# Two-stage kernel (mLSTM cell, then hash routing): output gates as exp(-o) inside the divisor, and a prologue whose first gate rows move within SBUF

## The chip, the cores and the metric

The kernel runs on one core of a Trainium2 chip. The metric is the device time of one launch in microseconds (us); the kernel before takes 426.49 us (median of three runs, 426.43 to 426.7). Its profiled execution spans 423.8 us on the core.

Engine names in the profile: PE is TensorE (matmul), PEld its weight load, DVE is VectorE, ACT is ScalarE, POOL is GpSimd, SP is SyncE, which here only issues DMAs. A name with q (ACTq, SPq) is an engine's queue when it issues a DMA.

## The reference

Two blocks in a row. The first is an mLSTM cell over 4 batches, 8 heads, 768 time steps and head width 40; the second sends each of the 3072 rows to one of 8 experts (two matmuls with a ReLU between), chosen by a hash of the token's id.

```python
for t in range(S):
    m_new  = np.maximum(f_gate[:, :, t] + m, i_gate[:, :, t])
    f_stab = np.exp(f_gate[:, :, t] + m - m_new)
    i_stab = np.exp(i_gate[:, :, t] - m_new)
    m = m_new
    C = f_stab * C + i_stab * outer(v_t, k_t)        # per head, 40 x 40
    n = f_stab * n + i_stab * k_t
    h_tilde = C @ q_t
    denom = np.maximum(np.abs(n . q_t), 1.0)
    o = 1.0 / (1.0 + np.exp(-o_gate[:, :, t]))
    y[:, :, t] = o * h_tilde / denom
...
x = y.transpose(0, 2, 1, 3).reshape(B * S, H * D)    # 3072 x 320
out[rows of expert e] = np.maximum(x[rows] @ w1[e], 0) @ w2[e]
```

What matters here is the last line of the loop: the sigmoid of the output gate times the cell's output, divided by `denom`. Written out it is h_tilde / ((1 + exp(-o_gate)) * denom), one quotient.

## The kernel before

The time axis of the first block is cut into 24 steps `s` of 128 rows: 4 batches `b` with 6 chunks `c` each. In a step, TensorE turns k and q (transposes), computes the decay matrix from rows `R` and `L` of bf16 pieces (`decays`), the state (`state`), the scores q·k (`scores`) and the output (`attend`), and turns the output back (`back`); ScalarE takes the exp of the decays and copies PSUM to SBUF; VectorE weighs the scores; then `finish` divides and gates. The second block follows, TensorE's two large matmul loops (lines 836, 829 and 865 of the program). The program's order is each engine's order (`manual_schedule`).

The decay rows need the gates' running sums with full precision in bf16 operands, so each f32 row is split into three bf16 pieces. The pieces (`zA` for the decays A and exp(A), `zE` for the input side) are stored in DRAM and loaded back in the layout of `R` and `L`:

```python
def store_a(r, eng):   eng.dma_start(za_d[z_rows(r), :3, :], zA[r, :3, :])
def store_e(r, eng):   eng.dma_start(ze_d[z_rows(r)], zE[r])
def store_x(r, eng):   eng.dma_start(za_d[z_rows(r), 3:, :], zA[r, 3:, :])

def decays(s):
    ...
    for hf in range(2):
        ab = ps.tile([P, PR, P], F32, name="ab", tag="tr", bufs=4)
        for i in range(2):
            nc.tensor.matmul(ab[i * HB : (i + 1) * HB],
                lhsT=Ls[b % 2][:, c * P + i * HB : c * P + (i + 1) * HB],
                rhs=R[:, i, hf::2, :], start=True, stop=True)
        nc.scalar.activation(w[:, hf], ab[:], AF.Exp)

def sigmoid(s):
    o = og[s, "all"]                  # a group of 3 or 6 steps
    nc.scalar.activation(o, o, AF.Sigmoid)

def finish(s):
    d = st.pop(s)
    hs = d["xo"].rearrange("p f i (x d) -> p f (i x) d", d=DP)
    den = wk.tile([P, 2, PR, 1], F32, name="den")
    nc.vector.tensor_scalar(den[:], hs[:, :, :, D:D1], scalar1=-1.0, scalar2=1.0, op0=ALU.mult, op1=ALU.max)
    nc.vector.tensor_tensor(den[:], den[:], hs[:, :, :, D:D1], op=ALU.max)
    x = wk.tile([P, H, D], F32, name="x")
    xv = x.rearrange("p (j f) d -> p f j d", f=2)
    nc.vector.tensor_tensor(xv, hs[:, :, :, :D], og[s].rearrange("p (j f) d -> p f j d", f=2), op=ALU.mult)
    nc.vector.reciprocal(den[:], den[:])              # 128 x 8
    eng = nc.vector if s + 1 == NT else nc.gpsimd
    eng.tensor_tensor(xv, xv, den[:].to_broadcast([P, 2, PR, D]), op=ALU.mult)
    return lambda: nc.sync.dma_start(x_d[s * P : (s + 1) * P, :], x.rearrange("p h d -> p (h d)"))
```

The prologue (cut to its order): `g0` are 32 partitions with the first two chunks of all batches, `g1` 64 partitions with the other four.

```python
f_sb, i_sb <- gates (ACT queue);  k0, q0, k1, q1, v0, k2 (SP queue);  fP, iP (ACT queue)
tables()                                   # constant rows of R and L
scan of m, first 256 columns               # VectorE
turn_k(0); turn_q0(0)
load_q0(2), load_o(0), load_v(1), load_o(1), load_v(2), load_o(2)
scores(0)
gates(g0, ..., (G, G, G)); gates_e(g0, (A, A, A))     # pieces on GpSimd, ScalarE
store_a(g0, A); store_e(g0, A)
turn_k(1); turn_q0(1)
scan of m, the other 512 columns; m_sb -> mP by DMA
load_a(0, A); load_e(0, [0])               # R and L of step 0, from DRAM
gates_rest(g0, ...); store_x(g0, A)        # exp(A) and its pieces
...
gates_turn(g0); decays(0); entering(0); load_a(1, A); k_weights(0)
gates(g1, ...); weigh(0); ...; gates_e(g1, ...); store_a, store_e, gates_rest, store_x of g1
for s in range(NT): ...                    # the steps
```

Of the kernel before, what the change touches and what calls it, by code (L numbers as in the profile page):

```python
# [17 lines left out]
P = 128  # L18
# [4 lines left out]
def kernel(  # L23
# [93 lines left out]
    with tc.tile_pool(name="gates", bufs=1) as gp, \  # L117
# [48 lines left out]

        groups = [(0, 3)] + [(s, min(s + 6, NT)) for s in range(3, NT, 6)]
        og = {}

        def load_o(s):  # L170
            for s0, s1 in groups:
                if s == s0:
                    tile_o = ld.tile([P, 6, H, D], F32, name="og", bufs=2)
                    og[s, "all"] = tile_o[:, : s1 - s0]
                    for i in range(s0, s1):
                        og[i] = tile_o[:, i - s0]
            nc.sync.dma_start(og[s], rows_of(o_gate, s))

        def load_q(b, part):

            if part == 0:
                qb[b] = {"l": ld.tile([P, H, NB * D], F32, name="ql", bufs=2)}
            hs = slice(part * PR, (part + 1) * PR)
            nc.sync.dma_start(qb[b]["l"][:, hs], q[b, hs].rearrange("h (p r) d -> p h (r d)", r=NB))

# [19 lines left out]
        def pieces_of(z, i0, t, ra, rb, r, eng):  # L205
            for j, piece in enumerate((hi(t[r]), hi(ra[r]), rb[r])):
                if eng[j] is nc.scalar:
                    nc.scalar.copy(z[r, i0 + j, :], piece)
                else:
                    nc.gpsimd.tensor_copy(z[r, i0 + j, :], piece)  # L210

        def gates(rows, m0, m1, f, i, eng):

            r = rows
            first = r.start == 0
            nc.vector.tensor_add(aP[r], f, m0)
            nc.vector.tensor_sub(aP[r], aP[r], m1)
            if first:
                nc.vector.memset(aP[r, 0:1], 0.0)
            nc.gpsimd.tensor_tensor(iP[r], i, m1, op=ALU.subtract)  # L220
            nc.vector.tensor_tensor_scan(AP[r], keep[r], aP[r], 0.0, op0=ALU.mult, op1=ALU.add)
            nc.vector.tensor_tensor(r1[r], AP[r], hi(AP[r]), op=ALU.subtract)
            nc.vector.tensor_sub(iP[r], iP[r], AP[r])
            nc.vector.tensor_tensor(r2[r], r1[r], hi(r1[r]), op=ALU.subtract)
            pieces_of(zA, 0, AP, r1, r2, r, eng)
# [4 lines left out]
        def gates_e(rows, eng):  # L230
            r = rows
            nc.vector.tensor_tensor(r3[r], iP[r], hi(iP[r]), op=ALU.subtract)
            nc.vector.tensor_tensor(r4[r], r3[r], hi(r3[r]), op=ALU.subtract)
            pieces_of(zE, 0, iP, r3, r4, r, eng)

        def store_a(r, eng):
            eng.dma_start(za_d[z_rows(r), :3, :], zA[r, :3, :])
# [4 lines left out]
        def store_x(r, eng):  # L242
            eng.dma_start(za_d[z_rows(r), 3:, :], zA[r, 3:, :])

        def gates_rest(rows, eng):
            r = rows
            Ac = AP[r].rearrange("p (c t) -> p c t", t=P)
            n = r.stop - r.start
            nc.vector.tensor_tensor(
                aP[r].rearrange("p (c t) -> p c t", t=P), iP[r].rearrange("p (c t) -> p c t", t=P),  # L250
                Ac[:, :, P - 1 : P].to_broadcast([n, 2, P]), op=ALU.add,
            )
            nc.scalar.activation(fP[r], AP[r], AF.Exp)
            nc.scalar.activation(aP[r], aP[r], AF.Exp)
            nc.vector.tensor_tensor(r1[r], fP[r], hi(fP[r]), op=ALU.subtract)
            nc.vector.tensor_tensor(r2[r], r1[r], hi(r1[r]), op=ALU.subtract)
            pieces_of(zA, 3, fP, r1, r2, r, eng)
# [83 lines left out]
        def sigmoid(s):  # L341
            o = og[s, "all"]
            nc.scalar.activation(o, o, AF.Sigmoid)
# [81 lines left out]

        def finish(s):
            d = st.pop(s)
            hs = d["xo"].rearrange("p f i (x d) -> p f (i x) d", d=DP)
            den = wk.tile([P, 2, PR, 1], F32, name="den")
            nc.vector.tensor_scalar(  # L430
                den[:], hs[:, :, :, D:D1], scalar1=-1.0, scalar2=1.0, op0=ALU.mult, op1=ALU.max,
            )
            nc.vector.tensor_tensor(den[:], den[:], hs[:, :, :, D:D1], op=ALU.max)
            x = wk.tile([P, H, D], F32, name="x")
            xv = x.rearrange("p (j f) d -> p f j d", f=2)
            nc.vector.tensor_tensor(
                xv, hs[:, :, :, :D], og[s].rearrange("p (j f) d -> p f j d", f=2), op=ALU.mult,
            )
            nc.vector.reciprocal(den[:], den[:])  # L439
            eng = nc.vector if s + 1 == NT else nc.gpsimd  # L440
            eng.tensor_tensor(xv, xv, den[:].to_broadcast([P, 2, PR, D]), op=ALU.mult)  # L441
            return lambda: nc.sync.dma_start(x_d[s * P : (s + 1) * P, :], x.rearrange("p h d -> p (h d)"))
# [172 lines left out]
        first_turns = {1: (0,), 2: (1,), 3: (2,), 4: (3, 4), 5: (5,)}  # L615
# [26 lines left out]
        flat = {id(t): src.rearrange("b h s -> (b h) s") for t, src in ((f_sb, f_gate), (i_sb, i_gate), (fP, f_gate), (iP, i_gate))}  # L642
        nc.scalar.dma_start(f_sb[:], flat[id(f_sb)])
        nc.scalar.dma_start(i_sb[:], flat[id(i_sb)])
# [6 lines left out]
        load_q0(1)  # L651
        load_v(0)
        load_k(2)
        for i in (1, 2):
            for t in (fP, iP):
                nc.scalar.dma_start(t[at[i] : at[i] + BH, :], flat[id(t)][:, i * W2 : (i + 1) * W2])
        nc.vector.memset(m_sb[:, 0:1], 0.0)
        tables()
        for t in [ks[2], kws[0]]:
            nc.gpsimd.memset(t[:, :, D:], 0.0)  # L660
        nc.vector.memset(keep[:], 1.0)
        nc.vector.memset(keep.rearrange("p (c t) -> p c t", t=P)[:, :, 0:1], 0.0)
        g0, g1 = slice(0, BH), slice(2 * BH, 4 * BH)
        A, G = nc.scalar, nc.gpsimd
# [3 lines left out]
        turn_k(0)  # L668
        turn_q0(0)
        load_q0(2)  # L670
        load_o(0)
        load_v(1)
        load_o(1)
        load_v(2)
        load_o(2)
        scores(0)
        gates(g0, m_sb[:, :W2], m_sb[:, 1 : W2 + 1], f_sb[:, :W2], i_sb[:, :W2], (G, G, G))
        gates_e(g0, (A, A, A))
        store_a(g0, A)
        store_e(g0, A)  # L680
        turn_k(1)
        turn_q0(1)
        nc.vector.tensor_tensor_scan(
            m_sb[:, W2 + 1 :], f_sb[:, W2:], i_sb[:, W2:], m_sb[:, W2 : W2 + 1], op0=ALU.add, op1=ALU.max,
        )
        for i in (1, 2):
            nc.scalar.dma_start(mP[at[i] : at[i] + BH, :], m_sb[:, i * W2 : (i + 1) * W2 + 1])
        load_a(0, A)
        load_e(0, [0])
        gates_rest(g0, (G, G, G))  # L690
        store_x(g0, A)
        nc.gpsimd.memset(Rs[1][32:HB], 0.0)
        for r in (slice(0, 32), slice(HB, P)):
            nc.sync.dma_start(Rs[1][r], Rs[0][r])
        for t in vs:
            nc.gpsimd.memset(t[:, :, D1:], 0.0)
            nc.gpsimd.memset(t[:, :, D:D1], 1.0)
        load_q(1, 0)
        load_q(1, 1)
# [307 lines left out]
```

## Time and profile before

| | before |
|---|---|
| time, median of 3 | 426.49 us |
| span of the profiled execution | 423.8 us |
| first block (to the first matmul of line 924) | 165.1 us |
| scores (sp) of steps 0, 1, 2 start at | 9.60, 29.31, 38.05 us |
| a step of the first block after that | 5.0 to 6.9 us |
| ACT_TABLE_LOAD | 5 before Sigmoid, 5 before the next Exp, 1 at the start; 1.28 us each |
| DVE reciprocal, 128x8 | 24 of 0.193 us |
| POOL product x·den, 128x320 | 23 of 0.724 us |

In the profile's second part the span is cut into 40 slices of 10.6 us; each digit is an engine's busy share in tenths. In the table of stretches each engine has its busy time in us, with the number of its instructions in brackets, then come the granted clock of TensorE as a share of full speed, the mean busy share of the 16 DMA engines, and GB/s. In the timeline a row has start and duration in us, engine, line, operation, and in square brackets the idle time ahead of it with what ended that. In a list of groups a row has the line, engine, operation, tiles, shapes and count; then the busy time in us and the mean of one in ns; then idle time and what ended it.

### The profile page before, as it was taken

The page shows a single profiled execution, that of the slowest core. Times are in us where ns is not written, and L with a number is a line of the kernel's source. Part 1 is how long each engine was busy: PE and PEld are TensorE (multiplying, and loading weights), DVE is VectorE, ACT ScalarE, POOL GpSimd, SP SyncE. Part 2 cuts the span into 40 slices and gives each one's busy share as a digit, 9 for nine tenths or more (in the row PEclk, how much of TensorE's full clock was granted, in tenths as well). Part 3 has the DMA queues.
Part 4 walks back from the last instruction along what each step waited for, and adds up shares of the span by engine and source line. Part 5 has one row for each costly group of instructions (what it writes and reads, how often), then busy time and mean ns, then how long its engine had stood idle before and what let it go on. Part 6 is the DMA issues. An engine that isn't in the chain of part 4 may idle for free.

```text
span 423.8 us, 7461 instructions
## 1 busy us (share of the span) xinstructions
PE 392.1 (93%) x2892; PEld 262.1 (62%) x2892; DVE 136.2 (32%) x373; ACT 134.3 (32%) x238; POOL 117.7 (28%) x202
## 2 busy tenths in 40 slices
PE   2369999999999997999999999999999999999992
PEld 2247877877887874556657556556556566575551
DVE  7364748776675762220120110210110201201100
ACT  5158786696495471010111111110111101111010
POOL 6364313313433421711402401311302212020021
PEclk9988999999999999999999999999999999999998
DMA  9829998899675630548508217144126100000000
GB/s 173 212 61 177 205 206 188 191 207 223 153 163 126 162 95 33 151 147 254 168 26 263 87 62 224 63 125 160 60 96 185 62 17 29 0 17 30 0 18 30
DMA packets 111784, 51.37 MB, mean 121 GB/s; under 512 B 86624, under 2 KB 105892, under 8 KB 111748
## 3 DMA queue, kind: packets, MB, share of 16 engines
q1 hardware_dynamic: 105898, 39.31, 38.2%
q0 software_dynamic: 2496, 8.20, 6.0%
q10 hardware_dynamic: 3354, 3.37, 2.4%
q8 instruction: 23, 0.38, 0.4%
q14 instruction: 13, 0.11, 0.1%
HBM read 42.00 MB, written 8.63 MB: 119 GB/s over the span
## 4 chain that ended last, share of the span: by engine, by line
PE 84%; ACT 5%; issue 5%; POOL 2%; DVE 1%; ACTq 1%; DMA 1%; POOLq 0%; DVEq 0%
PE mh L836 22%; PE zp L865 21%; PE sp L351 7%; PE ht L409 6%; PE mh L829 6%; PE ht L402 3%; PE mh L924 3%; PE ab L311 2%; PE tr L275 2%; PE xo L424 2%; PE ht L382 2%; PE tr L288 2%; PE tk L589 2%; PE tp L811 1%; PE xb L323 1%
## 5 line engine op out<-in xcount | busy, mean ns | idle before, releaser
L865 PE MATMUL zp<-w2t,h 128*128 128x320 f32 x384 | 105.2, 433 | 0.0
L836 PE MATMUL mh<-xT,w1t 128*128 128x416 f32 x256 | 96.2, 519 | 0.5 <-issue 0.5
L865 PEld LDWEIGHTS zp<-w2t,h 128*128 128x128 f32 x384 | 72.7, 190 | 32.1 <-issue 3.3
L836 PEld LDWEIGHTS mh<-xT,w1t 128*128 128x128 f32 x256 | 46.7, 190 | 42.7 <-issue 41.6
L817 DVE COPY xT<-tp 128x384 f32<-128x384 f32 x16 | 8.9, 558 | 141.4 <-PE tp L813 98.1
L798 POOL DMA_INDIRECT out_dram<-zo,s_idx x26 | 25.7, 988 | 92.5 <-ACT zo L797 92.5
L845 ACT ACTIVATE h<-mh 128x416 f32<-128x416 f32 x32 | 16.6, 517 | 107.4 <-PE mh L829 54.7
L797 ACT COPY zo<-zp 128x320 f32<-128x320 f32 x26 | 11.1, 426 | 101.1 <-PE zp L865 92.9
L843 DVE TENSOR_SCALAR h<-mh 128x416 f32<-128x416 f32 x32 | 18.9, 592 | 52.1 <-PE mh L829 26.3
L359 DVE TENSOR_TENSOR w<-sp,w 128x512 f32<-128x512 f32 x48 | 30.9, 686 | 13.7 <-PE sp L351 10.3
L441 POOL TENSOR_TENSOR x<-x,den 128x320 f32<-128x320 f32 x23 | 16.6, 724 | 61.6 <-DVE den L439 29.6
L351 PE MATMUL sp<-qT,kT 64*128 64x128 f32 x384 | 29.7, 297 | 4.1 <-ACT qT L289 4.1
L351 PEld LDWEIGHTS sp<-qT,kT 64*128 64x128 f32 x384 | 24.9, 199 | 10.7 <-ACT qT L289 5.9
L315 ACT ACTIVATE w<-ab 128x512 f32<-128x512 f32 x48 | 26.8, 614 | 4.6 <-PE ab L311 4.6
L409 PE MATMUL ht<-w,v 128*64 128x128 f32 x384 | 27.1, 285 | 0.0
L791 POOL DMA_INDIRECT xg<-x_rows,g_idx x24 | 23.4, 974 | 12.6 <-issue 12.6
L829 PE MATMUL mh<-xT,w1c 64*128 64x416 f32 x128 | 26.7, 535 | 0.0
L952 POOL COPY hrem<-h 128x256 f32<-128x256 f32 x8 | 3.2, 400 | 81.9 <-ACT h L845 81.9
L417 ACT COPY hT<-ht 128x512 f32<-128x512 f32 x24 | 14.1, 587 | 31.2 <-PE ht L409 31.2
L409 PEld LDWEIGHTS ht<-w,v 128*64 128x64 f32 x384 | 21.2, 140 | 4.0 <-issue 3.1
L289 ACT COPY qT<-tr 128x512 f32<-128x512 f32 x24 | 22.9, 977 | 0.6 <-PE tr L288 0.3
L275 PE MATMUL tr<-ident,k 128*128 128x128 f32 x96 | 17.4, 309 | 4.1 <-POOL R L638 4.1
(181 smaller groups left out, 421.3 us busy)
## 6 DMA issues: line engine op xcount, KB each, us to landing
w2t<-in_moe_w_dram SPq DMA_DIRECT2D x28, 320.0 KB
w1t<-in_moe_w_dram SPq DMA_DIRECT2D x28, 256.0 KB
k<-in_k_dram SPq DMA_DIRECT2D x24, 160.0 KB
v<-in_v_dram SPq DMA_DIRECT2D x24, 160.0 KB
og<-in_o_gate_dram SPq DMA_DIRECT2D x24, 160.0 KB
x_rows<-x SPq DMA_DIRECT2D x24, 160.0 KB
ql<-in_q_dram SPq DMA_DIRECT2D x6, 480.0 KB
w1c<-in_moe_w_dram SPq DMA_DIRECT2D x14, 128.0 KB
```

The source lines that it names most:

```text
L275: nc.tensor.transpose(tp[:, j, :], d["k"][:, 2 * j : 2 * j + 2, :].rearrange("p h d -> p (h d)"), ident[:])
L289: nc.scalar.copy(qb[b]["T"][:, :, cols], tp[:])
L315: nc.scalar.activation(w[:, hf], ab[:], AF.Exp)
L351: nc.tensor.matmul(sp[hf][:, j, :], lhsT=d["kT"][r, j, :], rhs=q_of(s)[r, j, :], start=True, stop=True,)
L359: nc.vector.tensor_tensor(d["w"][:, hf], d["sp"][hf][:], d["w"][:, hf], op=ALU.mult)
L409: nc.tensor.matmul(place(j, hf), lhsT=d["v"][:, 2 * j + hf, :], rhs=d["w"][:, hf, j, :], start=(c == 0 and j0 == 0), stop=True, skip_group ...
L791: nc.gpsimd.indirect_dma_start(out=xg, out_offset=None, in_=x_d[:, :], in_offset=bass.IndirectOffsetOnAxis(ap=idx, axis=0),)
L798: ins = nc.gpsimd.indirect_dma_start(out=out[:, :], out_offset=bass.IndirectOffsetOnAxis(ap=idx, axis=0), in_=zo[:], in_offset=None, bound ...
L829: nc.tensor.matmul(hp[i][:, :cols], lhsT=w1c[r, fp, :], rhs=xT[r, 2, :cols], start=first, stop=not first,)
L836: nc.tensor.matmul(hp[i][:, :cols], lhsT=w1t[:, db, fb * P : (fb + 1) * P], rhs=xT[:, db, :cols], start=(first and db == 0), stop=(not fir ...
L843: nc.vector.tensor_relu(h[:, 2 * fp, :cols], hp[i][:, :cols])
L865: nc.tensor.matmul(zp[:], lhsT=h[:, fb, j * P : (j + 1) * P], rhs=w[2][:, fb, :], start=(fb == 0), stop=(fb == FB - 1),)
```

## The change

It has two parts. The first is about the **output gate**. Instead of a Sigmoid on a group of three or six steps, each step takes exp(-o) on ScalarE, GpSimd adds 1 and multiplies by `denom`, VectorE takes the reciprocal of the whole 128x320 tile and multiplies the cell's output by it. Exp is the function that the decays use as well, so ScalarE keeps one table. The gates are loaded one step at a time, three steps ahead, in five buffers.

The second is the **prologue**. Step 0's pieces go from `zA` and `zE` straight into `R` and `L` by nine small DMAs within SBUF (`direct`); the DRAM copy serves only the later steps. exp(A) of `g0` is taken earlier, all six of its pieces are stored at once, loads that step 0 and 1 do not need come later, batch 1's queries are loaded in steps 0 and 1 and turned in steps 2 to 5 (before: steps 1 to 5), all pieces of `g1` are copied on GpSimd, and TensorE gets idle matmuls (`spin`, 6 + 22 + 5) at three places, whose result nobody reads.

```diff
         def load_o(s):
-            for s0, s1 in groups: ...                      # a tile of six steps, two buffers
-            nc.sync.dma_start(og[s], rows_of(o_gate, s))
+            og[s] = ld.tile([P, H, D], F32, name="og", bufs=5)
+            nc.sync.dma_start(og[s][:], rows_of(o_gate, s))
+        def direct():
+            for j in range(3):
+                for i in range(2):
+                    nc.sync.dma_start(Rs[0][32 + j : 33 + j, i], zA[:H, j, :P])
+            for j in range(3):
+                nc.scalar.dma_start(Ls[0][j : 3 * H : 3, :W2], zE[:H, j, :])
...
+        def spin(n):
+            t = ps.tile([P, 2, 512], F32, name="ht")
+            for _ in range(n):
+                nc.tensor.matmul(t[:, 1, :P], lhsT=ident[:], rhs=ident[:], start=True, stop=True)
...
-        def sigmoid(s):
-            o = og[s, "all"]
-            nc.scalar.activation(o, o, AF.Sigmoid)
+        def gate(s):
+            nc.scalar.activation(og[s][:], og[s][:], AF.Exp, scale=-1.0)
+            nc.gpsimd.tensor_scalar(og[s][:], og[s][:], scalar1=1.0, scalar2=None, op0=ALU.add)
...
+        def divisor(s):
+            ...                                            # den as before: max(|n.q|, 1), 128 x 8
+            o = og[s]
+            eng = nc.vector if s + 1 == NT else nc.gpsimd
+            eng.tensor_tensor(o[:], o[:], den[:].to_broadcast([P, H, D]), op=ALU.mult)
         def finish(s):
-            ...                                            # x = hs * o; den = 1 / den; x = x * den
+            hs = st.pop(s)["hs"]
+            o = og.pop(s)
+            nc.vector.reciprocal(o[:], o[:])
+            x = wk.tile([P, H, D], F32, name="x")
+            ov, xv = (t.rearrange("p (j f) d -> p f j d", f=2) for t in (o, x))
+            nc.vector.tensor_tensor(xv, hs[:, :, :, :D], ov, op=ALU.mult)
+            nc.sync.dma_start(x_d[s * P : (s + 1) * P, :], x.rearrange("p h d -> p (h d)"))
...
-        first_turns = {1: (0,), 2: (1,), 3: (2,), 4: (3, 4), 5: (5,)}
+        first_turns = {2: (0,), 3: (1,), 4: (2, 3), 5: (4, 5)}
...
+        spin(6)
         turn_k(0)
         turn_q0(0)
-        load_q0(2) load_o(0) load_v(1) load_o(1) load_v(2) load_o(2); scores(0)
-        gates(g0, ...); gates_e(g0, ...); store_a(g0, A); store_e(g0, A)
+        gates_a(g0, ...); A.activation(fP[g0], AP[g0], AF.Exp); gates_b(g0, A)
+        load_q0(2); load_v(1)
+        direct()
+        A.activation(aP[g0], aP[g0], AF.Exp)
+        gates_x(g0)
         turn_k(1)
         turn_q0(1)
+        store_a(g0, A)
+        scores(0)
+        spin(22)
...
-        load_a(0, A); load_e(0, [0]); gates_rest(g0, ...); store_x(g0, A)
...
         decays(0)
         entering(0)
         load_a(1, A)
-        gates(g1, ..., (G, A, G)); weigh(0); gates_e(g1, ...); store_a, store_e, gates_rest, store_x
+        gates_a(g1, ...); A.activation(fP[g1], AP[g1], AF.Exp); gates_b(g1, G); gates_x(g1)
+        weigh(0)
...
         for s in range(NT):
...
                 back(s - 1)
-                store = finish(s - 1)
+                divisor(s - 1)
+            if s == 0:
+                spin(5)
             if s + 1 < NT: decays(s + 1)
+            if s == 0: store_a(g1, A); store_e(g1, A); store_e(g0, nc.sync)
-            if s > 0 and (s, "all") in og: sigmoid(s)
+            gate(s)
             state(s)
             if s + 1 < NT:
                 entering(s + 1)
+                if s == 0: A.activation(aP[g1], aP[g1], AF.Exp); load_a(2, A); load_e(0, [1, 2])
                 k_weights(s + 1)
-            if s > 0: store()
+            if s > 0: finish(s - 1)
+            if s + 3 < NT: load_o(s + 3)
             if s + 1 < NT: scores(s + 1); weigh(s + 1)
```

(Lines joined by semicolons stand on lines of their own in the program.)

## The prediction

> **What bounds the kernel now.** I read the page first: shares, slices, clock.
>
> ```profile
> PE 392.1 (93%) x2892; PEld 262.1 (62%) x2892; DVE 136.2 (32%) x373; ACT 134.3 (32%) x238; POOL 117.7 (28%) x202
> ...
> PE   2369999999999997999999999999999999999992
> DVE  7364748776675762220120110210110201201100
> ACT  5158786696495471010111111110111101111010
> ```
>
> One slice is 10.6 us. TensorE is full from slice 5 to the end, so after about 42 us only less TensorE work or fewer TensorE waits can pay, and the change removes no matmul that the result needs. The slack lies in the first four slices. The second view is the table of stretches of 4 us (columns: length, then busy us of PE, PEld, DVE, ACT, POOL, granted clock, DMA share, GB/s):
>
> ```profile
> 8.00:12.00 4.00, 2.40 (x18) 2.17 (x19) 3.62 (x7) 2.57 (x6) 1.53 (x3) 1.00 1.11 194
> 12.00:16.00 4.00, 1.58 (x8) 1.18 (x6) 0.00 (x0) 1.17 (x2) 0.00 (x0) 1.00 0.92 183
> 16.00:20.00 4.00, 0.42 (x2) 0.28 (x2) 1.93 (x5) 0.72 (x2) 2.16 (x4) 1.00 1.03 302
> 20.00:24.00 4.00, 3.43 (x15) 2.02 (x17) 2.12 (x5) 1.58 (x4) 3.46 (x12) 1.00 0.31 60
> 24.00:28.00 4.00, 1.29 (x20) 1.06 (x19) 3.56 (x8) 1.65 (x5) 1.71 (x3) 1.00 0.11 27
> 28.00:32.00 4.00, 3.25 (x24) 2.59 (x25) 2.17 (x5) 2.31 (x6) 3.48 (x13) 0.51 0.38 88
> ```
>
> From 12 to 20 us TensorE works 2.0 us of 8 and every engine idles at 12 to 16: the gates' pieces are travelling to DRAM and back. The third view, the timeline, names the wait:
>
> ```profile
> 16.28 0.31 ACTq L188 DMA_DIRECT2D L<-input_pieces  x1
> ...
> 20.57 1.07 PE L311 MATMUL ab<-R,L 128*64 128x512 bf16 x4 [2.75 <-DMA L<-input_pieces]
> ...
> 29.31 2.08 PE L351 MATMUL sp<-qT,kT 64*128 64x128 f32 x16
> ...
> 38.05 1.16 PE L351 MATMUL sp<-qT,kT 64*128 64x128 f32 x16
> ```
>
> The pieces are stored at 10.24 and 10.66, loaded back from 15.15, and step 0's decay matmuls start only at 20.57. The scores (sp) of step 1 start at 29.31, of step 2 at 38.05; then a step takes 5.0 to 6.1 us. The same 16 sp matmuls take 2.08 us at 29.31 and 1.16 at 38.05: early TensorE runs at about half speed. A fourth view, stretches cut from one sp to the next, shows what Sigmoid costs:
>
> ```profile
> 50.03:56.97 6.94, 6.41 (x89) 4.93 (x88) 4.16 (x12) 6.89 (x9) 2.28 (x4) 1.00 0.77 184
> ...
> 78.53:83.97 5.44, 5.44 (x84) 4.40 (x84) 4.17 (x13) 3.24 (x7) 1.86 (x4) 1.00 0.91 228
> 83.97:90.03 6.06, 5.64 (x85) 4.37 (x84) 4.18 (x13) 6.01 (x8) 1.81 (x4) 1.00 0.71 167
> ```
>
> In the two steps with a Sigmoid ScalarE is busy nearly throughout (6.89 of 6.94, 6.01 of 6.06) and TensorE stands still for 0.53 and 0.42; a plain step has no gap.
>
> **What the Trainium skill says.** "TensorE: Matmul & The Clock Gate", Part 1: the array starts at half clock, and a busy window of about 3.4 us releases it. The trace agrees (2.08 against 1.16 us; granted clock 0.51 at 28 to 32); this is what the new idle matmuls are for. "ScalarE: Activation LUTs", Table sets: exp and sigmoid lie in different sets, so alternating costs a table load each way. Agrees: ten loads around the Sigmoids, but of 1.28 us each, not the page's 2.7. "DMA: Bandwidth & Descriptors", Anatomy of one DMA: most of a DMA's fixed cost of about 2 us is the receipt that the data landed; a store and a load in a row pay twice, and one copy once. The trace has 9.9 us from the piece store's issue to the matmul. "VectorE: DVE Perf Modes", Walkthrough of the 8-slice pipeline: reciprocal is an iterative divide with a repeat count of 8. The trace shows it on 8 elements only, below.
>
> **The change, part by part.**
>
> *1, prologue.* The chain up to the pieces is untouched: the scan starts at 5.02, when the input gate lands, and the last difference (L233) ends at 10.1. ScalarE copies kT and qT until 9.55; then come the new early exp (0.41) and three zE copies about 0.35 apart, to about 11.1, and three issues of about 0.35, to 12.2. How long does such a copy take to land? The step-1 load into R took 1.2 us from the end of its second issue (22.39) to the matmul (23.53) with the DMA engines idle; the L load took 4.0 (16.59 to 20.57) with them full. The queue is half drained by then, so I take 2.5: operands at 14.7. TensorE must first get through the idle matmuls. The 22 records of L924 (11 matmuls of 416 columns) take 7.92 us, 0.72 each, so 128 columns take 0.22, and 22 of them 4.9 us at full clock. Behind scores that end at about 11, they end at 16. So decays(0) moves from 20.57 to about 16. Step 1's R comes by the next load: issued behind the two exp of w, at about 17.3, landing at 19.5 to 20.5. But the order of instructions puts weigh(0) on VectorE behind the whole of g1's chain, and scores(1) needs the score banks that weigh(0) empties. g1 starts when mP lands, about 15.8, and has 11 VectorE operations of 0.42 to 0.69: 5.4 us, to 21.2. weigh(0) takes 1.29, so scores(1) starts at about 22.5 instead of 29.31. Step 2's operands: GpSimd copies g1's nine pieces by itself, 0.40 to 0.66 each, 17.4 to about 22.8; store, 2 us; load, 2 us or more; decays(2) at 27.5 to 28.5, scores(2) at 29 to 30.5. Against 38.05 that is **about -8 us**, -6 to -10, half-clock time saved included.
>
> *2, Sigmoid to exp.* The first group (s = 0) lies inside part 1. Of the others, s = 3 cost about 1.0 us (6.94 against 5.92 for its neighbours with as many matmuls) and s = 9 0.6 (6.06 against 5.44); s = 15 nothing (6.09 between 6.10 and 5.69), s = 21 little. The new exp on 128x320 takes about 0.42 (fP, 256 wide: 0.41); added to ScalarE's 3.2 us in a plain step of 5.4 that is hidden. **-1.6 us.**
>
> *3, batch 1's queries.* Its turns move from steps 1 to 5 with (1,1,1,2,1) to steps 2 to 5 with (1,1,2,2). Step 5 gets a second copy of 1.0 us, which scores(6) waits for; step 1 loses a turn of 0.44. **+0.6 us.**
>
> *4, the divisor.* Per step GpSimd keeps one 128x320 product (0.72) and gains an addition, about 0.4 to 0.5; it goes from 2.1 to 2.6 us of 5.5: hidden. VectorE keeps its product (0.49) and trades a reciprocal of 8 elements for one of 320:
>
> ```profile
> L439 DVE RECIPROCAL den<-den 128x8 f32<-128x8 f32 x24 | 4.6, 193 | 0.0
> ...
> L430 DVE TENSOR_SCALAR den<-xo 128x8 f32<-128x8 f32 x24 | 4.0, 167 | 24.1 <-PE xo L424 24.1
> L433 DVE TENSOR_TENSOR den<-den,xo 128x8 f32<-128x8 f32 x24 | 3.9, 163 | 0.8
> ```
>
> It takes 193 ns where other operations on 8 elements take 163 to 167. If these 27 ns are a fixed latency, 320 elements take 0.49 + 0.03 = 0.52 us (a). If they grow with the elements, 3.4 ns each, 0.49 + 1.08 = 1.57 us (b). If every element takes 8 cycles, which I infer from the page's repeat count and its 0.96 GHz, 320 take 2.67, with overhead 2.8 us (c), an estimate. One place speaks against (c): at 151.51 a reciprocal starts and the next operation starts 0.11 us later, where independent operations with 8 elements are 0.08 apart and eight times 8 cycles would add about 0.06. I give (a) 40%, (b) 45%, (c) 15%. VectorE's mean is 3.66 us a step; less 0.19 it becomes 4.0, 5.0 or 6.3 against steps of 5.0 to 6.1: no drag; about 0.2 a step where the route adds work, +3 to +4 in all; or the bound, +0.6 to +1 a step, about +18. At the middle of these chances **+1.5 us**. After the last step it is on the path alone: **+0.5 us**.
>
> Sum: -8 - 1.6 + 0.6 + 1.5 + 0.5 = -7.0; 426.49 - 7.0 = 419.5.
>
> **The rivals.** *VectorE becomes the bound*: case (c) gives 426.5 - 8.5 + 18 = 436; for it, the repeat count and the 27 ns, against it the 0.11 us. *The DMA engines take it back*: their share is 0.9 to 1.0 from 38 to 70 us, so an earlier start could meet loads that aren't there. Against: they stand at 0.31 and 0.11 at 20 to 28, room that the new order of loads uses. If it happens, the gain shrinks to about 4: 422. *A new wait replaces the DRAM trip*: g1's nine pieces on GpSimd alone, or the 22 idle matmuls at half clock (9.7 us, to 21). That leaves 3 to 5 of the 8 us: 423. *Everything is hidden*: not credible, as no engine was full at 12 to 20.
>
> **Range and chances.** With (a) and a good prologue (-10) it is 415 to 416; with (b) 420 to 423; with (c) 432 to 438. The range that should hold eight times in ten is 412.5 to 430. The 2% line is at 418.0, which case (a) just reaches and (b) needs luck for: faster 0.38, within 2% 0.52, slower 0.10.
>
> **What would show it.** Decay matmuls of step 0 at about 16 us with sp at 1.1 us instead of 2.1; scores(1) at 22 to 23 and scores(2) at 29 to 30.5, released by weigh(0) and by the DMA of step 2's pieces; only one table load in the first 160 us; the 320-wide reciprocal at 0.5, 1.6 or 2.8 us, and in the last case TensorE waiting for VectorE in every step; a longer step before scores(6). I am wrong if the reciprocal is (c), or if scores(2) starts later than 33.

## The result and the profile after

The changed kernel takes **453.72 us** (median of 4 runs, 452.58 to 455.04) against 426.6 us of the kernel before beside it: a ratio of 1.0634 [1.0596, 1.0671]. It is slower by 27 us, far above the predicted range of 412.5 to 430. The profiled execution spans 452.9 us, against 423.8.

Shares and slices of the page of the kernel after:

```profile
PE 405.2 (89%) x2958; PEld 271.2 (60%) x2958; DVE 184.5 (41%) x374; ACT 124.2 (27%) x243; POOL 143.0 (32%) x229
...
PE   8697878787889899499999999999999999999993
DVE  7767777887788899812102011020020110200100
```

The kernel before had TensorE at 9 from slice 4 on, but for one 7 at the end of its first block and the last slice. Now a slice is 11.3 us and TensorE stands mostly at 7 to 9 up to slice 16; in slice 17 (the 4) the first block ends. VectorE's row has risen instead. Its busy time grew by 48.3 us (136.2 to 184.5) with one instruction more. The groups of the page (busy us and mean ns of one, then the idle time before) name it:

```profile
L445 DVE RECIPROCAL og<-og 128x320 f32<-128x320 f32 x24 | 51.5, 2147 | 3.8 <-POOL og L440 3.6
```

24 of them take 51.5 us; the 8-wide ones of the kernel before took 4.6. The table of stretches (length; busy us and count of PE, PEld, DVE, ACT, POOL; clock; DMA share; GB/s) shows one step, from the start of one step's scores to the next, s = 15, first before and then after:

```profile
111.75:117.86 6.11, 6.11 (x90) 5.07 (x88) 4.17 (x13) 3.25 (x8) 2.42 (x5) 1.00 0.55 130
```

```profile
129.09:136.36 7.27, 6.25 (x90) 5.00 (x88) 6.03 (x13) 3.70 (x8) 3.44 (x6) 1.00 0.62 135
```

The same 90 matmuls take about the same 6.1 to 6.2 us, but the step lasts 7.27: TensorE waits for 1.0 us. And yet VectorE is not full either (6.03 of 7.27). No engine is the bound of this step; the chain of waits of the kernel after shows what is. Columns: start, us, what.

```profile
129.31 0.68 DVE qs L329
129.99 2.07 DVE og L445
...
132.50 1.28 DVE w L361 x2
133.77 0.24 DVE qp L282
...
134.15 0.63 PE tr L290 x4
134.78 0.44 PE xo L426 x4
135.22 0.55 PE ab L313 x4
135.77 0.47 PE ht L384 x16
...
136.34 0.22 DVE C L390
...
136.58 0.68 DVE qs L329
```

The chain begins and ends with the same instruction, 7.27 us apart: it is a **loop through the order of two engines**. The reciprocal (og) stands in VectorE's order between the scaling of the queries (qs) and the weighing of the scores (w); behind w comes the padding of a query row for the next batch (qp, `pad_q`); TensorE turns that row (tr) before it may begin the next step's xo, ab and state matmuls (ht); those feed C and qs. The 2.07 us lie in the middle of this ring, and each link of it waits for the one ahead. It is not the width alone that put them there: before, at the start of the step shown, the product (110.87 us) and the narrow reciprocal (111.28) stood ahead of C (111.67) and qs (111.91); the change has moved both behind qs. In the list of waits of the kernel before there is no wait of the turns for qp; after it is this line (us in total, times, longest):

```profile
PE tr L290 <- DVE qp L282: 20.6, 14, 2.2
```

The last batch supports the reading: it has no next batch whose queries must be padded, and its steps 18 to 21 last 6.28, 5.78, 6.12 and 6.09 us against 5.62, 5.02, 5.62 and 5.62 before, only 0.5 to 0.8 more. The two longest steps, from scores(7) to scores(8) and from scores(13) to scores(14), take 8.80 and 8.78 us; in these the granted clock was 0.81.

The prologue did what it was meant to do. TensorE's timeline after (start, us, line, operation; in brackets the idle time before it and its releaser):

```profile
14.75 0.89 PE L313 MATMUL ab<-R,L 128*64 128x512 bf16 x4 [0.66 <-DMA L<-zE]
...
23.34 2.67 PE L353 MATMUL sp<-qT,kT 64*128 64x128 f32 x16 [2.88 <-DVE w L361]
...
31.39 1.16 PE L353 MATMUL sp<-qT,kT 64*128 64x128 f32 x16
```

Step 0's decays start at 14.75 instead of 20.57, the scores of step 1 at 23.34 instead of 29.31 and those of step 2 at 31.39 instead of 38.05. So the span of 29.1 us more is the sum of three stretches: -6.7 us up to scores(2); +29.8 us from scores(2) to scores(23) (118.87 before, 148.70 after), 1.42 us a step; and +5.9 us from scores(23) to the second block's first zp matmul (36.7 before, 42.6 after). From there to the end both kernels take 230.2 us.

### The profile page after: what moved, and what is told of

Same layout as the page of the kernel before. It is cut to its first block, busy times and chain, and to the rows that moved or that the text cites. A ratio compares the mean times of both kernels' runs of the same rounds, so it can differ in the third digit from the quotient of the medians.

```text
span 452.9 us, 7646 instructions
## 1 busy us (share of the span) xinstructions
PE 405.2 (89%) x2958; PEld 271.2 (60%) x2958; DVE 184.5 (41%) x374; ACT 124.2 (27%) x243; POOL 143.0 (32%) x229
## 4 chain that ended last, share of the span: by engine, by line
PE 68%; DVE 19%; issue 6%; POOL 2%; DMA 1%; ACT 1%; ACTq 1%; POOLq 0%; DVEq 0%; SPq 0%
PE mh L847 20%; PE zp L876 20%; DVE og L445 7%; DVE w L361 6%; PE mh L840 6%; PE sp L353 3%; PE ht L411 3%; PE mh L935 3%; PE tr L290 2%; PE ab L313 2%; PE xo L426 2%; PE ht L384 2%; PE tp L822 1%; PE ht L404 1%; PE tr L277 1%
## 5 line engine op out<-in xcount | busy, mean ns | idle before, releaser
L445 DVE RECIPROCAL og<-og 128x320 f32<-128x320 f32 x24 | 51.5, 2147 | 3.8 <-POOL og L440 3.6
L290 PE MATMUL tr<-ident,qp 128*128 128x128 f32 x96 | 15.5, 290 | 23.3 <-DVE qp L282 20.6
L440 POOL TENSOR_TENSOR og<-og,den 128x320 f32<-128x320 f32 x23 | 16.6, 722 | 52.2 <-DVE den L437 52.2
L345 POOL TENSOR_SCALAR og<-og 128x320 f32<-128x320 f32 x24 | 24.2, 1009 | 15.1 <-ACT og L344 13.3
L290 PEld LDWEIGHTS tr<-ident,qp 128*128 128x128 f32 x96 | 11.0, 148 | 27.1 <-ACT kT L278 18.6
```

Of the source, the lines that this page charges most:

```text
L290: nc.tensor.transpose(tp[:, j, :], t[:, 2 * j : 2 * j + 2, :].rearrange("p h d -> p (h d)"), ident[:])
L345: nc.gpsimd.tensor_scalar(og[s][:], og[s][:], scalar1=1.0, scalar2=None, op0=ALU.add)
L445: nc.vector.reciprocal(o[:], o[:])
```

## The experiments

Start of the scores (sp) in us, in the profiled execution of each kernel; "layer 2" is the second block's first zp matmul. A column is one execution, and executions differ: up to scores(2) e9 (below) and e6 have the same instructions, and start them at 32.05 and 30.72. The columns of e1 and e7 come from the slowest of their kernels' runs (427.13 and 423.60 us).

| scores of step | before | after | e1 | e2 | e3 | e4 | e5 | e6 | e7 | e8 |
|---|---|---|---|---|---|---|---|---|---|---|
| 1 | 29.31 | 23.34 | 25.19 | 23.51 | 29.51 | 23.30 | 29.07 | 23.05 | 23.22 | 23.54 |
| 2 | 38.05 | 31.39 | 34.62 | 32.55 | 37.86 | 31.49 | 37.27 | 30.72 | 34.18 | 31.85 |
| 3 | 44.04 | 38.92 | 41.37 | 41.75 | 45.23 | 40.14 | 43.20 | 37.55 | 41.01 | 38.25 |
| 6 | 62.44 | 62.00 | 60.10 | 61.92 | 67.38 | 62.14 | 61.00 | 56.26 | 59.73 | 58.33 |
| 13 | 100.50 | 113.05 | 98.28 | 101.03 | 118.02 | 104.83 | 98.40 | 93.64 | 97.11 | 100.79 |
| 23 | 156.92 | 180.09 | 155.07 | 157.57 | 183.73 | 167.75 | 154.84 | 150.06 | 153.54 | 159.14 |
| layer 2 | 193.61 | 222.67 | 195.15 | 197.23 | 226.69 | 211.18 | 191.28 | 186.66 | 191.71 | 199.25 |

Each time below stands beside the kernel before on the same chip: 428.11 us for e1 to e4, 426.45 for e5 to e8, 427.57 for e9 to e11, 426.88 for e12. Ratios are to that, with their 95% intervals.

**e1: the reciprocal on 8 elements.** The changed kernel, whole, but 312 of each row's 320 quotients are left out:

```diff
-            nc.vector.reciprocal(o[:], o[:])
+            nc.vector.reciprocal(o[:, 0, 0:8], o[:, 0, 0:8])
```

> The changed kernel with the reciprocal cut to the first 8 of its 320 columns; the other 312 quotients are left out, everything else stays. Theory A (the wide reciprocal, 2.145 us on VectorE in every step, is the whole loss): the first block is bound by TensorE again, steps of 5.0 to 6.1 us, and with the prologue's 6.7 us kept the time is 416 to 420. Theory B (the chain den, GpSimd product, GpSimd addition of 1.008 us instead of the 0.45 assumed is what delays the step): the reciprocal's width matters little, 445 or more. Theory C (the gates loaded step by step, or the new prologue's loads, starve the steps): 445 or more as well.

Measured: 424.07 us, ratio 0.9889 [0.9849, 0.9929]. The operation takes 0.197 us instead of 2.147, and this one line turns 6% slower into 1% faster. From scores(2) to scores(23) it takes 120.45 us instead of 148.70: 28.25 us, 1.35 a step. Everything else of the new gate, the exp on ScalarE, the addition and the product on GpSimd, is still there and costs no more than the prologue brings. So the loss is the width of this reciprocal. The time is above the 416 to 420 that were expected: in the execution profiled, scores(2) start at 34.62 instead of 31.39, with the same prologue, so not every execution has the 6.7 us gained there.

**e2: the new prologue with the old gate.** Groups of six steps, Sigmoid and the old `finish` are put back:

```diff
-            nc.scalar.activation(og[s][:], og[s][:], AF.Exp, scale=-1.0)
-            nc.gpsimd.tensor_scalar(og[s][:], og[s][:], scalar1=1.0, scalar2=None, op0=ALU.add)
+            nc.scalar.activation(o, o, AF.Sigmoid)       # o: a group of 3 or 6 steps
...
-            nc.vector.reciprocal(o[:], o[:])
+            nc.vector.reciprocal(den[:], den[:])
```

> The new prologue with the old output gate (Sigmoid on groups, reciprocal on 8 elements, product on GpSimd). Theory A: 419 to 421, that is before less the 6.7 us by which the scores of step 2 start earlier in the changed kernel, with steps as before. Theory C (the prologue's new order of loads and turns costs the steps): 426 or more.

Measured: 426.72 us, 0.9953 [0.9928, 0.9977], over 20 runs that spread from 423.4 to 431.5. Scores(2) start at 32.55, 5.5 us early, but scores(3) only at 41.75, 2.3 early. The chain of waits of e2:

```profile
33.17 5.15 DMA ql<-in_q_dram
...
38.34 0.34 DVE qp L288
...
38.81 0.63 PE tr L296 x4
```

The first turn of batch 1 waits for its query rows, which the DMA engines bring at 38.31. So here a transfer ate 3.2 of the 5.5 us: in this mixture the grouped gate loads stand ahead of the queries. e12 takes up this cause. Another 2.9 us go between scores(3) and scores(23), 115.82 us against 112.88 before.

**e3: the new gate with the old prologue.** The gate, divisor and `finish` of the change, nothing else, here against the kernel before:

```diff
-            nc.scalar.activation(o, o, AF.Sigmoid)
+            nc.scalar.activation(og[s][:], og[s][:], AF.Exp, scale=-1.0)
+            nc.gpsimd.tensor_scalar(og[s][:], og[s][:], scalar1=1.0, scalar2=None, op0=ALU.add)
...
-            nc.vector.reciprocal(den[:], den[:])
+            nc.vector.reciprocal(o[:], o[:])
```

> The old prologue with the new output gate. If the two parts add up, as theory A has it: 426.6 plus 34 (the loss of 27 plus the 6.7 won in the prologue), 457 to 462, with the 320-wide reciprocal at 2.145 us and steps of about 7.3 us. If the early start is what collides (theory C), less: 440 to 450.

Measured: 461.08 us, 1.078 [1.072, 1.0841]. With the old prologue the gate alone costs 33 us; the prologue then gives back 6 to 7 of them (461.08 to 453.72 us on different chips; by the ratios 0.0146, or 6.2 us). The loss is the gate's, not the prologue's, and not the meeting of the two.

**e4: the loop cut.** The padding of the next query rows is put ahead of the reciprocal in VectorE's order; the work stays the same:

```diff
+            nb = b + (c == NB - 1)
+            if nb + 1 < B and s + 1 < NT:
+                for r in (turns_of if nb else first_turns).get((c + 1) % NB, ()):
+                    pad_q(nb + 1, r)
             ...
                 finish(s - 1)
             ...
-            nb = b + (c == NB - 1)
-            if nb + 1 < B and s + 1 < NT: ...   # pad_q stood here, behind finish and weigh
```

> The changed kernel with one move in VectorE's order: the copy that pads the next batch's queries (0.24 us, for which TensorE's turn in the next step waits) goes ahead of the reciprocal instead of behind the weighing of the scores. Work and counts stay. If the loss is a loop of waits through the order (pad, turn, xo, decays, state, C, qs, reciprocal, product, weigh, pad: 7.27 us in steps 15 to 17), steps fall to what VectorE has to do, 5.7 to 6.2 us, and the time to 438 to 444. If VectorE's sheer work is the bound already, it stays within 2 us of 453.7.

Measured: 442.82 us, 1.0329 [1.0287, 1.0372]. If VectorE's busy time were the bound, its order could not matter; it is worth 11 us, or 13 by the two ratios. The same step of e4 in the table of stretches, and its chain:

```profile
118.34:125.09 6.75, 6.24 (x90) 5.05 (x88) 5.93 (x13) 3.70 (x9) 3.35 (x6) 1.00 0.64 141
```

```profile
122.47 0.59 ACT kT L278
123.06 1.00 ACT qT L291
...
124.10 0.41 PE ab L313 x2
```

This step falls from 7.27 to 6.75 (5.7 to 6.2 were expected) with the same VectorE work (5.93). Its chain now runs through TensorE and ScalarE's copies of kT and qT; the reciprocal has left it. So the ring is shown, but it is not the whole loss: from scores(2) to scores(23) e4 takes 136.26 us, 12.4 less than the changed kernel, where e1 takes 28.25 less. In step 2 (8.65 us) the padding, now ahead of the reciprocal, waits for query rows until 36.55 us and holds up VectorE; step 3 (8.67) ends in a wait for a load of R, until 47.39. And in some steps VectorE is nearly full after all, as from scores(11) to scores(12), where it is busy for 7.03 of 7.24 us:

```profile
91.78:99.02 7.24, 4.93 (x67) 3.77 (x65) 7.03 (x16) 3.29 (x8) 1.80 (x2) 1.00 0.99 230
```

How the rest of the 15.8 us divides, no run here shows.

**e8: the reciprocal at half its width.** 160 of 320 elements, the other quotients left out:

```diff
-            nc.vector.reciprocal(o[:], o[:])
+            nc.vector.reciprocal(o[:, : PR], o[:, : PR])
```

> The changed kernel with the reciprocal on 160 of its 320 columns (the other quotients are left out). If its time grows with the elements, as 193 ns for 8 and 2145 for 320 suggest (6.26 ns each, 0.14 fixed), it takes 1.14 us, and a step with a turn falls from 7.27 to about 6.3. If it were a step function of the shape, 2.1 or 0.2.

Measured: 431.25 us, a single run, and by tile (min, median and max ns) first e8, then the kernel after:

```profile
L445 DVE RECIPROCAL og<-og x24: 1144/1146/1155, 32.7 to 167.4; 128x160 f32<-128x160 f32 x24
```

```profile
L445 DVE RECIPROCAL og<-og x24: 2143/2145/2153, 32.2 to 189.7; 128x320 f32<-128x320 f32 x24
```

(2145 - 1146) / 160 = 6.24 ns for each element, and 2145 - 320 x 6.24 = 148 ns fixed. On 8 elements that gives 0.198 us, and 0.197 was measured: the duration is linear over these three widths. Most steps with a turn take 6.27 us, so even a reciprocal of 1.15 us costs time: from scores(2) to scores(23) it is 127.29 us, 6.8 more than in e1.

**e5 and e6: a gate without a wide reciprocal.** The sigmoid is (1 + tanh(o/2))/2. ScalarE takes the tanh, VectorE multiplies by (1 + tanh) in the one pass in which it forms the product anyway, and the 2 goes into the divisor, whose reciprocal stays 8 wide. The gates are loaded a step at a time, as in the change. e5 does it on the old prologue, e6 on the new one. Here against the kernel before:

```diff
-            nc.scalar.activation(o, o, AF.Sigmoid)
+            nc.scalar.activation(og[s][:], og[s][:], AF.Tanh, scale=0.5)
...
-                den[:], hs[:, :, :, D:D1], scalar1=-1.0, scalar2=1.0, op0=ALU.mult, op1=ALU.max,
+                den[:], hs[:, :, :, D:D1], scalar1=-1.0, scalar2=2.0, op0=ALU.mult, op1=ALU.max,
...
-            nc.vector.tensor_tensor(
-                xv, hs[:, :, :, :D], og[s].rearrange("p (j f) d -> p f j d", f=2), op=ALU.mult,
-            )
+            for f in range(2):
+                nc.vector.scalar_tensor_tensor(
+                    xv[:, f], in0=ov[:, f], scalar=1.0, in1=hs[:, f, :, :D], op0=ALU.add, op1=ALU.mult,
+                )
...
-            nc.gpsimd.memset(t[:, :, D:D1], 1.0)
+            nc.gpsimd.memset(t[:, :, D:D1], 2.0)
```

> The old prologue with the gate written as sigmoid(o) = (1 + tanh(o/2)) / 2: ScalarE takes tanh per step, VectorE forms (tanh + 1) * h in two operations of half the columns, the ones column of v becomes 2 so that the divisor carries the half, the reciprocal stays on 8 elements, GpSimd multiplies by it. No wide reciprocal; no table load if tanh sits in exp's set. Theory A: the cost goes and the Sigmoid gaps go as well (1.6 us in steps 3 and 9, up to 2.3 in step 0): 422 to 425 against 426.6. If a gate step by step costs by itself (loads, GpSimd), 427 or more.

> The same gate on the new prologue. Theory A: what the wide reciprocal run with 8 columns gave (a ratio of 0.989) or a little better, as GpSimd's addition is gone too: ratio 0.980 to 0.989. If the prologue's gain is lost again in the steps, as in the run with the prologue alone, it is no better than the old prologue with tanh.

Measured: e5 423.27 us, 0.9929 [0.9906, 0.9953]; e6 **419.36 us**, 0.9831 [0.9807, 0.9854]. Both beat the kernel before, and of the other kernels only e9 (below) is as fast as e6. Three lines from the groups of e6 say what the gate now costs:

```profile
L439 DVE SCALAR_TENSOR_TENSOR x<-og,xo 128x160 f32<-128x160 f32 x48 | 13.2, 317 | 0.0
L442 DVE RECIPROCAL den<-den 128x8 f32<-128x8 f32 x24 | 4.7, 196 | 0.0
L635 ACT ACT_TABLE_LOAD x1 | 1.3, 1283 | 1.9 <-issue 1.9
```

Two passes of 0.317 us and a reciprocal of 0.196 take the place of one pass of 0.49 and one of 2.147, and the whole program has one table load. e6 against e5 is what the prologue is worth when nothing spoils it: scores(2) 6.55 us earlier, scores(3) 5.65, scores(6) 4.74, scores(23) 4.78, and 3.9 us of time. The losses on the way are step 2 (6.83 us against 5.93; e9, which starts it 1.33 us later, takes 5.93) and the step before scores(6) (6.43 against 5.52), where batch 1's turns now stand closer together.

**e7: e6 without the 33 idle matmuls.**

```diff
-        spin(6)
...
-        spin(22)
...
-                spin(5)
```

> The tanh gate on the new prologue without the 33 idle matmuls of the prologue. If they hold the clock up where it counts, this is 1 to 4 us slower than with them, with sp of step 0 at 2.1 us instead of 1.1. If the prologue is bound by DMA and VectorE, and the clock falls again in the waits before step 1 (granted 0.50 at 24 to 28 us in the changed kernel, idle matmuls and all), there is no difference beyond 1 us.

Measured: 421.34 us, 0.9873 [0.9851, 0.9896]; the idle matmuls are worth 2.0 us by the medians, and every run of e7 is above every run of e6. How they earn them the trace does not settle. Up to scores(1) nothing is lost without them (23.22 us against 23.05), though the sp of step 0 take 1.45 us instead of 1.16. Scores(2) start at 34.18 instead of 30.72, behind this wait in the timeline of e7:

```profile
30.27 0.58 ACT L418 COPY hT<-ht 128x512 f32<-128x512 f32 x1 [4.05 <-DMA input_pieces<-zE]
...
30.90 1.11 PE L425 MATMUL xo<-ident,hT 128*128 128x128 f32 x4 [3.28 <-ACT hT L418]
```

The store of g1's pieces, issued at 23.65 us, lands at 29.83; in e6 it is issued at 23.53 and lands at 26.69. TensorE then goes on at a lower clock. The table of stretches of e7:

```profile
32.00:36.00 4.00, 4.00 (x39) 3.07 (x38) 1.92 (x7) 1.72 (x4) 2.67 (x10) 0.50 1.13 225
```

Granted clock 0.50, and the 16 sp matmuls take 2.06 us instead of 1.16. In e6 the clock of these same 4 us is 1.00. From xo to scores(2) it is 3.28 us, in e6 2.35 (28.37 to 30.72). So in this execution 2.5 of the 3.5 us come ahead of xo, with the late store, and 0.9 behind it, with the clock. Whether the idle matmuls have to do with the store is not shown.

**e9: batch 1's turns spread otherwise.** e6, with the second turn one step earlier:

```diff
-        first_turns = {2: (0,), 3: (1,), 4: (2, 3), 5: (4, 5)}
+        first_turns = {2: (0,), 3: (1, 2), 4: (3, 4), 5: (5,)}
```

> The tanh gate on the new prologue, with batch 1's six turns in steps 2 to 5 as 1, 2, 2, 1 instead of 1, 1, 2, 2. In the tanh runs the scores of step 6 start 6.43 us after those of step 5, where the old prologue has 5.52, because two copies of qT stand ahead of them. If that is the cause, this step falls to 5.5 and the time by 0.5 to 0.9 us, as step 3 gets a second turn of 0.44 that TensorE has to do anyway. If the loads of batch 1 are late instead, step 3 waits for them and nothing is won.

Measured: 419.70 us, 0.9818 [0.9792, 0.9844]: not to be told from e6. The step from scores(5) to scores(6) is 5.53 us instead of 6.43, as the double turn has gone from it; but the step from scores(3) to scores(4) is 6.84 instead of 5.93. The 0.9 us goes where the second turn goes.

**e10: weigh(0) ahead of the rest of g1's chain.** e9, with one line moved:

```diff
+        weigh(0)
         gates_x(g1)
-        weigh(0)
```

> The run with turns 1, 2, 2, 1, and weigh(0) moved ahead in VectorE's order, from behind the eleven operations of g1's chain to behind the first three. The prediction said that scores(1) (23.05 us) waits for it. If so, scores(1) starts at about 20.5 to 21.5. Step 2's operands come through g1's chain, which now stands 1.3 us later, so scores(2) (30.72) should not gain and may lose up to 1.3: the time stays within 1 us of the run with turns 1, 2, 2, 1.

Measured: 422.04 us, 0.9871 [0.9827, 0.9914]. Scores(1) start at 20.93 instead of 23.39: that weigh(0) held them is shown. But scores(2) start at 33.06 instead of 32.05. The chain of e10 leads from there back through the DRAM trip of g1's pieces (24.4 to 31.9 us) to their copies on GpSimd: g1's work, moved back behind weigh(0), is what step 2 waits for. By the medians this order is 2.3 us slower than e9's (1 at most was expected), but the intervals of the two ratios overlap; what is shown is that the earlier scores(1) bring nothing.

**e11: the first rows through DRAM after all.** e6, where the nine small transfers within SBUF are replaced by a store and two loads, as before:

```diff
-        direct()
+        A.dma_start(za_d[z_rows(g0), :3, :], zA[g0, :3, :])
+        store_e(g0, A)
+        load_a(0, A)
+        load_e(0, [0])
...
-        store_a(g0, A)
+        A.dma_start(za_d[z_rows(g0), 3:, :], zA[g0, 3:, :])
...
-                store_e(g0, nc.sync)
```

> The tanh gate on the new prologue, with the first rows taken through DRAM again (store, then load, on ScalarE's queue) instead of by nine copies within SBUF; the idle matmuls stay. If the trip was what held step 0, its decay matmuls go from 14.5 back to 18 to 20.5 us, and since ScalarE takes g1's exp behind them, the scores of step 2 go from 30.7 to 33 to 35 and the time rises by 2 to 4 us. If g1's chain on VectorE and GpSimd is the bound anyway, step 0 moves and step 2 and the time do not.

Measured: 425.68 us, 0.9957 [0.9937, 0.9976]. The direct way is worth some 5 us (0.9957 less 0.9831 is 1.3% of 427), more than expected, and not where I expected it. TensorE's timeline of e11:

```profile
14.60 0.62 PE L313 MATMUL ab<-R,L 128*64 128x512 bf16 x4 [0.40 <-DMA L<-input_pieces]
```

Step 0's decays start at 14.60 us even with the trip through DRAM. It is 4.0 us from the store's issue (10.58) to the matmul, where the kernel before needed 10.3 (10.24 to 20.57). The load's issue and ScalarE's queue ahead of it tell half of the reason, first before, then e11:

```profile
13.68 1.38 ACTq L687 DMA_DIRECT2D mP<-m_sb  x2
15.15 1.03 ACTq L199 DMA_DIRECT2D R<-decay_pieces  x2
```

```profile
12.26 0.78 ACTq L200 DMA_DIRECT2D R<-decay_pieces  x2
```

Before, the load is issued 4.9 us after the store, behind the two transfers of mP; in e11 1.7 us after it, as the new prologue issues mP from SyncE's queue. That is 3.2 of the 6.3 us. The other 3.1 lie between the load's issue and the matmul (5.4 us before, 2.3 in e11), and there the DMA engines differ; the stretch from 12 to 14 us, before and in e11:

```profile
12.00:14.00 2.00, 1.58 (x8) 1.18 (x6) 0.00 (x0) 0.97 (x2) 0.00 (x0) 1.00 0.98 222
```

```profile
12.00:14.00 2.00, 1.53 (x15) 1.34 (x14) 1.27 (x2) 0.57 (x2) 1.86 (x6) 1.00 0.08 20
```

The DMA engines' share is 0.98 there before, and 0.08 in e11; from 16 to 20 us, where the load of before is under way, it is 1.03. So with mP's transfers and the loads that are not needed yet out of the way, the trip through DRAM takes 4.0 us, and step 0 starts as early as with `direct` (14.46 in e6). No run takes the two apart. What `direct` saves comes a step later: the store that step 1 waits for is issued at 13.29 us in e6 and at 15.90 in e11, step 1's load at 15.44 and 19.56. Step 1's decays start at 19.51 and 22.45, scores(1) at 23.05 and 25.11. Scores(2), at 30.72 and 36.52, lose 3.7 us more; the chain of e11 leads from there to a load of k (24.85 to 30.58) and one of L (30.60 to 34.24), so to transfers again.

**e12: batch 1's queries first.** e2, with both loads at the head of step 0, ahead of the values and the grouped gates:

```diff
+            if s == 0:
+                load_q(1, 0)
+                load_q(1, 1)
             if s + 3 < NT:
                 load_v(s + 3)
...
-            if s < 2:
-                load_q(1, s)
```

> The new prologue with the old gate once more, but batch 1's query loads (two of 480 KB) issued together at the head of step 0 instead of one each in steps 0 and 1 behind two gate loads each. In the run with the prologue alone TensorE waited for the second of them until 38.3 us, and the scores of step 3 started at 41.75, only 2.3 us before the old kernel's 44.04. If this collision ate the prologue's gain, step 3 starts at 38 to 39.5, and the ratio falls from 0.995 to 0.985 to 0.990. If the DMA engines are short of time altogether, another load is late instead (v of step 3, the gates), and the ratio stays at 0.993 or more.

Measured: 423.27 us, 0.9906 [0.9886, 0.9927], and scores(3) at 38.81 instead of 41.75. The cause found in e2 is confirmed for these 2.9 us; the ratio lies just outside the range expected.

## Why the prediction was wrong, point by point

**Part 4, the reciprocal: the step that failed.** It failed twice. The first failure is the size. Of the three sizes I gave 0.52 us 40%, 1.57 us 45% and 2.8 us 15%; it is 2.145, between (b) and (c). Case (b) took a difference of 27 ns between unlike operations, and multiplied it by 40; it got 3.4 ns an element on top of an ordinary pass of 0.49 us. The two points of e8 put 6.24 ns on each element and leave 148 ns fixed, so the 8 elements had cost 50 of their 193 ns, not 27. Case (c) took 8 cycles an element from the repeat count of 8 in the Trainium skill ("VectorE: DVE Perf Modes", Walkthrough: the 8-slice pipeline in each mode); the page gives a count and no duration. By an estimate with that page's clock of 0.96 GHz the measured 6.24 ns are 6.0 cycles. The piece of evidence I put against (c), a next operation starting 0.11 us after a reciprocal of 8 elements, could not bear its weight: it says when the next operation starts, not when a wide one ends.

The second failure is the way in which the cost was counted. I set VectorE's busy time per step against the length of a step, and even case (c) gave only 0.6 to 1 us a step. The measured size lies below (c), and the loss above it: 1.35 us a step by e1. In most steps the bound was not a sum but a ring through VectorE's and TensorE's order, on which the added 1.95 us (2.145 less 0.196) lie in full. e4 shows it by moving one instruction out of the ring: 12.4 of the 28.25 us come back. With the reciprocal on 8 elements the ring would have about 5.3 us (7.27 less 1.95, an estimate from the chain), less than the 6.11 of TensorE's own work, so no view of the kernel before could show it. Once the ring is cut, VectorE's sum does count in some steps (7.03 of 7.24 us in e4), so the sum was incomplete rather than void.

Nor was the +1.5 us put in for the divisor the mean of the chances given: 0.45 x 3.5 + 0.15 x 18 is +4.3, which makes the forecast 422.3. Neither sign that was named for being wrong came true: the reciprocal is below (c), and scores(2) start before 33.

**Part 4, GpSimd's addition:** mis-sized, 1.009 us instead of 0.4 to 0.5, but hidden as predicted: e1 has it, and is faster than the kernel before.

**Part 1, the prologue: right in kind, too large.** Decays(0) at 14.75 (predicted about 16), sp of step 0 at 1.16 us, scores(1) at 23.34 (22.5) behind weigh(0), scores(2) at 31.39 (29 to 30.5): -6.66 instead of -8. A term that did not come is the saving of half-clock time in step 1: from 24 to 28 us the clock is again at 0.50 and its scores take 2.67 us, after TensorE has waited 2.88 us for weigh(0). The reason that I gave, the trip through DRAM, was half wrong: by e11 the trip takes 4.0 us once the transfers in its way are gone, so these held step 0; what the direct way saves shows in steps 1 and 2.

**Part 2, Sigmoid to exp:** no experiment takes it alone. e5, which also has one activation a step and one table load and the old prologue, gains 3.2 us: 0.8 us of it up to scores(2) and 2.1 up to scores(23), so about 1.3 between, near the 1.6 predicted. Of the 1.0 us that I read off for s = 3 (6.94 us), only 0.58 were the Sigmoid's: the same step takes 6.36 in e5, which keeps its double turn. The exp takes 0.472 us (0.42 predicted).

**Part 3, batch 1's queries:** the double turn costs 0.9 us in its step (e9), as against 0.6 predicted on balance.

**The sum without the divisor** was -9.0 us. e6, which has all of it but another gate, gives -7.1: the other terms together were 1.9 us too hopeful. That the forecast of 419.5 is e6's time is chance.

**The rivals.** "VectorE becomes the bound" had the right engine, and for most steps the wrong mechanism. "The DMA engines take it back" happens in e2. "A new wait replaces the trip" did not come true for step 0; for step 2 the chain of e6 runs back through g1's copies on GpSimd (from 18.10 us), their store and load, so there it holds.

**The stretch from scores(23) to the first zp** grew by 5.9 us, and its two parts have different causes. Up to the second block's first matmul it is 8.2 us before, 8.3 in e5, 9.1 in e1 and 12.4 in the changed kernel: +4.2, with three wide reciprocals in the chain there (from 181.05, 186.10 and 189.68 us). So the +0.5 us that the prediction gave for the end was too small as well: e1 against the changed kernel makes it 3.3. From that matmul to the first zp it goes with the granted clock (the column ahead of the DMA share), first before, then after:

```profile
165.14:193.61 28.47, 27.99 (x100) 15.13 (x101) 6.31 (x18) 2.88 (x6) 10.00 (x11) 1.00 0.45 144
```

```profile
192.50:222.67 30.17, 30.01 (x99) 16.05 (x100) 6.03 (x17) 2.88 (x6) 9.98 (x11) 0.93 0.44 136
```

It is 28.2 us in e5 and 28.3 in e6 (clock 1.00), but 31.0 in e1 (0.95) and 29.9 in e7 (0.94), whose second blocks have the same work. Why the clock is lower in some executions is open. Times here are therefore compared by their intervals and not by single traces.

## What to carry to other kernels

Folding a division into an operand's whole width made this reciprocal eleven times as long (0.196 to 2.145 us); measure such an operation at the width in question before trading a table function for it, and look first for a form that keeps the division narrow, such as tanh in place of sigmoid. An engine with time to spare can still set the pace: follow the chain of waits until an instruction comes round again, and see whether the new operation falls into that ring; if so, its length counts as soon as the ring is longer than the work of the busiest engine, or the order must change. And before a round trip through DRAM is taken out, look at what stands ahead of it in its queue and at the DMA share while it runs: these may be the real cost.

## What the runs showed of the hardware that I had not expected

- VectorE's reciprocal on f32 in SBUF takes 0.148 us + 6.24 ns per element of a row (8, 160 and 320 elements: 0.197, 1.146, 2.145 us).
- GpSimd adds a constant to 128x320 f32 in 1.009 us, but multiplies the same shape by a second operand in 0.722 us: the operation with one input is the slower one.
- From the end of its last issue to the matmul, the load of step 0's pieces took 1.2 us in e11 (13.38 to 14.60; DMA share 0.21 from 12 to 16 us) and 4.0 us before (16.59 to 20.57; share 1.03 from 16 to 20 us).
- Without the 33 idle matmuls of the prologue the time is 2.0 us longer (e7), but they do not hold the clock for long: in the changed kernel it is granted at 0.50 again from 24 to 28 us, in e6 at 0.66, and in e7, without them, at 1.00.
